# The opening of an adaLN linear-attention and bilinear-GLU block: loads on two issuers, sums moved between VectorE and TensorE, the k product by parts

## The chip, the cores and the metric

The kernel runs on one core of one Trainium2 chip. A core has TensorE (PE in the profile; PEld is its weight load), VectorE (DVE), ScalarE (ACT), GpSimd (POOL) and SyncE (SP), which issues the transfers in the kernel before. The engines run beside each other and wait for one another through semaphores; each works through its own instructions in the order in which the program gives them. The metric is the device time of one execution in microseconds, as the median of several runs; less is better.

## The reference, cut to what matters

The input x has 2048 tokens of width 512. One conditioning vector c makes six vectors of width 512, of which the first two are the shift `sa` and the scale `ca` of the first layer norm:

```python
mod = (_silu(c) @ w_mod).reshape(c.shape[0], 6, 1, -1)
sa, ca, ga, sb, cb, gb = (mod[:, 0], mod[:, 1], mod[:, 2], mod[:, 3], mod[:, 4], mod[:, 5])
h = _layernorm(x, axis=-1) * (1 + ca) + sa
x = x + ga * _A_ref(h, A_wqkv, A_wo)          # linear attention: q, k, v = h @ wqkv, 32 heads of 16
h = _layernorm(x, axis=-1) * (1 + cb) + sb
x = x + gb * _B_ref(h, B_w_gate, B_w_up, B_w_down)   # ((h W) * (h V)) W2
```

So before any product of h with `wqkv` can start, there must be the statistics of x, the normalized x, and the sums over 512 rows of `w_mod` that give shift and scale. All is float32.

## The kernel before, in words

Tokens are taken in 4 chunks of 512; a chunk is 4 tiles of 128 tokens by 512 columns (256 KB each). The 512 columns are 4 blocks of 128, called k (of the inner dimension) or b (of shift and scale). All products are made in three parts to keep float32's accuracy: each operand is split into a high part (a rounded copy, made by ScalarE) and a low part (the rest, made by VectorE), and the product is high by high, high by low, low by high.

The order of all work is written out by hand (`manual_schedule`): what stands earlier in the program comes earlier on its engine. The opening, lines 127 to 521, does this for chunk 0:

- Loads. `load` (L109) takes one of 99 buffers and issues a transfer from SyncE. The order is: x tile 0, c, x tiles 1 to 3, scale blocks 0 and 1 (`raw_half[1, 0]`, two transfers), shift blocks 0 and 1 (`raw_half[0, 0]`), the first block of the k weight, scale blocks 2 and 3, shift blocks 2 and 3, the other k weight blocks, then x of chunk 1, the q and v weights and the other chunks.
- Fillers. `keep_on` (L152) makes matmuls on zeros while nothing else is there for TensorE.
- Norm. `stats` (VectorE), `rstd_of` (VectorE, then GpSimd), `nmr_of` (VectorE) and `xhat` (ScalarE, for tile 3 VectorE) normalize a tile; `transpose_token` (L281) turns it on TensorE, 4 blocks of 128 by 128, into 4 banks, one for each k.
- Shift and scale. A block's 128 sums over 512 rows are made in one of two ways. `block_pe` (L390): 4 matmuls with one column each, straight from the loaded rows. `half_dve` (L397) with `mod_acc` (L167): 4 operations of VectorE over two blocks at once, after which `block_one` (L402) adds over the partitions by a matmul with ones. Before, scale blocks 0 and 1 go by `block_pe`, all others by `half_dve`. `block_out` (L407) takes a block's shift and scale out of PSUM on VectorE. Block 1's sums lie in the bank of the fillers (`ps_idle`), the others' in `ps_m`.
- h. `mod_h` and `mod_f` (ScalarE) make the modulated block k twice, rounded and full; `mod_l` (VectorE) the difference. `weight_h` (ScalarE) and `weight_l` (VectorE) split the k weight.
- k product. `cells` (L439) issues the matmuls of token tile t, block k and the parts asked for: part 0 is h high by weight high, part 1 h high by weight low, part 2 h low by weight high; 4 x 4 x 3 = 48 in all, into a bank for each t. The bank of t = 2 is `ps_idle`; that of t = 3 is one that the transposes of k = 0 had.

The lines that set the order of the first cells before are:

```python
half_dve(0, 0, 0, 1, 2, 3)
weight_h(0)
n0.transpose_token(2)
n0.transpose_token(3)
keep_on(2)
block_one(0, 0)
block_out(0)
weight_l(0)
mod_h(0)
```

After the opening, TensorE makes q, the k products of the other chunks and the attention's sums, and then the second half with its gate, up and down products.

Of the kernel before, what the change touches and what calls it, by code (L numbers as in the profile page):

```python
# [9 lines left out]
F32R = mybir.dt.float32r  # L10
AF = mybir.ActivationFunctionType
# [3 lines left out]
P = 128  # L15
# [7 lines left out]
def tile_adaln_block(  # L23
# [12 lines left out]
    nc = tc.nc  # L36
# [3 lines left out]
    KD = D // P  # L40
    NJ = 4
# [8 lines left out]
    xv = x[0].rearrange("(c p j) d -> c j p d", p=P, j=NJ)  # L50
# [14 lines left out]
    def f32(ap):  # L65
        return ap.bitcast(F32)
# [3 lines left out]
    def T(p, tag, shape=(P, D), dt=F32, bufs=None):  # L70
        cnt[0] += 1
        return p.tile(list(shape), dt, tag="t" if p is tiles else tag, name=f"{tag}_{cnt[0]}", bufs=bufs)

    def B(tag, shape=(P, D), dt=F32):

        return T(tiles, tag, shape, dt)
# [29 lines left out]
    nc.gpsimd.memset(half, -0.5)  # L106


    def load(src, tag):  # L109
        raw = B(tag, (P, *src.shape[1:]))[:src.shape[0]]  # L110
        nc.sync.dma_start(raw, src)
        return raw

    def load_x(ch):
        return [load(xv[ch, j], "x") for j in range(NJ)]

    def load_mod(v):
        return [load(wm_v[:, k, v * D:(v + 1) * D], "raw") for k in range(KD)]

    def load_half(v, half):  # L120
        a = v * D + half * D // 2
        return [load(wm_v[:, k:k + 2, a:a + D // 2], "raw") for k in range(0, KD, 2)]
# [3 lines left out]

    xts = [[load(xv[0, 0], "x")]]
    ct = consts.tile([P, KD], F32, name="ct")
    nc.sync.dma_start(ct, c[0].rearrange("(p k) -> p k", k=KD))
    xts[0] += [load(xv[0, j], "x") for j in range(1, NJ)]  # L130
    raw_half = {}
    raw_half[1, 0] = load_half(1, 0)
    raw_half[0, 0] = load_half(0, 0)
    load_k = lambda k: load(wqkv_v[k, :, D:2 * D], "raw")
    raw_k = [load_k(0)]
    raw_half[1, 1] = load_half(1, 1)
    raw_half[0, 1] = load_half(0, 1)
    raw_k += [load_k(k) for k in range(1, KD)]
    xts.append(load_x(1))
    raw_q = load_qkv(0)  # L140
    raw_v = load_qkv(2)
# [10 lines left out]
    def keep_on(n):  # L152
        for _ in range(n):
            nc.tensor.matmul(ps_idle, idle[:, :P], idle, start=True, stop=True)
# [12 lines left out]
    def mod_acc(acc, raws, ks):  # L167
        for k in ks:
            if k == 0:
                nc.vector.tensor_scalar(acc, raws[k], sc[:, 0:1], None, op0=ALU.mult)  # L170
            else:
                nc.vector.scalar_tensor_tensor(acc, raws[k], sc[:, k:k + 1], acc, op0=ALU.mult, op1=ALU.add)
# [148 lines left out]
    def k_split_xh(i):  # L321
        ch, j = divmod(i, NJ)
        kx[i] = [B("xh", dt=F32R), B("xl", dt=F32R)]
        nc.scalar.activation(kx[i][0], norm[ch].n[j], AF.Copy)

    def k_split_xl(i):
        ch, j = divmod(i, NJ)
        nc.vector.tensor_tensor(kx[i][1], norm[ch].n[j], f32(kx[i][0]), op=ALU.subtract)
# [45 lines left out]
    n0 = norm[0]  # L374
    both = consts.tile([P, KD, 2], F32, name="both")
    ca, sa = both[:, :, 0], both[:, :, 1]
    ps_m = acc_bank()

    def half_of(v, b):

        pair = raw_half[v, b // 2]
        return [pair[k // 2][:, k % 2, b % 2 * P:(b % 2 + 1) * P] for k in range(KD)]

    def at_of(v, b):
        return 2 * b + 1 - v

    def sums_in(b):
        return ps_idle if b == 1 else ps_m

    def block_pe(v, b):  # L390
        at, ps = at_of(v, b), sums_in(b)
        for k, raw in enumerate(half_of(v, b)):
            nc.tensor.matmul(ps[:, at:at + 1], raw, sc[:, k:k + 1], start=k == 0, stop=k == KD - 1)
# [3 lines left out]
    def half_dve(v, half, *ks):  # L397
        if 0 in ks:
            sums[v, half] = B("f")[:, :D // 2]
        mod_acc(sums[v, half], [raw_half[v, half][k // 2][:, k % 2] for k in range(KD)], ks)  # L400

    def block_one(v, b):  # L402
        at = at_of(v, b)
        nc.tensor.matmul(sums_in(b)[:, at:at + 1], sums[v, b // 2][:, b % 2 * P:(b % 2 + 1) * P], ones,
                         start=True, stop=True)

    def block_out(b):  # L407
        nc.vector.tensor_tensor(both[:, b], sums_in(b)[:, 2 * b:2 * b + 2], unit, op=ALU.add)

    halves = {}  # L410

    def mod_h(k):
        halves[k] = (B("h", dt=F32R), B("h", dt=F32R), B("f"))
        h, l, f = halves[k]
        nc.scalar.activation(h, n0.ps[k], AF.Identity, scale=ca[:, k:k + 1], bias=sa[:, k:k + 1])

    def mod_f(k, on=None):
        h, l, f = halves[k]
        if on:
            on.tensor_scalar(f, n0.ps[k], ca[:, k:k + 1], sa[:, k:k + 1], op0=ALU.mult, op1=ALU.add)  # L420
        else:
            nc.scalar.activation(f, n0.ps[k], AF.Identity, scale=ca[:, k:k + 1], bias=sa[:, k:k + 1])
        n0.ps[k] = None

    def mod_l(k):
        h, l, f = halves.pop(k)
        nc.vector.tensor_tensor(l, f, f32(h), op=ALU.subtract)
        n0.t[k] = (h, l)

    def weight_h(k):  # L430
        wk.append((B("w", dt=F32R), B("w", dt=F32R)))
        nc.scalar.activation(wk[k][0], raw_k[k], AF.Copy)

    def weight_l(k, on=None):
        (on or nc.vector).tensor_tensor(wk[k][1], raw_k[k], f32(wk[k][0]), op=ALU.subtract)
# [3 lines left out]
    def cells(*tk, parts=(0, 1, 2)):  # L439
        for part in parts:  # L440
            for t, k in tk:
                h, l = halves[k][:2] if k in halves else n0.t[k]
                x, w = ((h, wk[k][0]), (h, wk[k][1]), (l, wk[k][0]))[part]
                nc.tensor.matmul(kps[t], x[:, t * P:(t + 1) * P], w, start=k == 0 and part == 0,  # L444
                                 stop=k == KD - 1 and part == 2)
# [7 lines left out]
    n0.stats(2)  # L453
    n0.nmr_of(0, 2)
    n0.xhat(0, 1)
    k_split_xh(0)
    n0.stats(3)
    n0.rstd_of(2, 4)
    n0.transpose_token(0)
    n0.nmr_of(2, 4)  # L460
    n0.xhat(2)
    n0.xhat(3, on=nc.vector)
    keep_on(2)
    n0.transpose_token(1)
    block_pe(1, 0)
    keep_on(1)
    half_dve(0, 0, 0, 1, 2, 3)
    weight_h(0)
    n0.transpose_token(2)
    n0.transpose_token(3)  # L470
    keep_on(2)
    block_one(0, 0)
    block_out(0)
    weight_l(0)
    mod_h(0)
    mod_f(0)
    block_pe(1, 1)
    block_one(0, 1)
    half_dve(1, 1, 0, 1)
    block_out(1)  # L480
    half_dve(1, 1, 2, 3)
    mod_l(0)
    kps.update({t: acc_bank() for t in range(2)})
    kps[2] = ps_idle
    kps[3] = bank()
    four = lambda k: [(t, k) for t in range(NJ)]
    cells((0, 0), (1, 0), parts=(0, 1))
    cells((2, 0), (3, 0), parts=(0, 1))
    cells(*four(0), parts=(2,))
    mod_h(1)  # L490
    mod_f(1)
    weight_h(1)
    half_dve(0, 1, 0, 1, 2, 3)
    weight_l(1)
    mod_l(1)
    k_split_xh(1)
    cells(*four(1), parts=(0,))
    block_one(1, 2)
    block_one(0, 2)
    block_one(1, 3)  # L500
    block_one(0, 3)
    cells(*four(1), parts=(1, 2))
    weight_h(2)
    block_out(2)
    block_out(3)
    weight_l(2)
    mod_h(2)
    mod_f(2)
    weight_h(3)
    mod_l(2)  # L510
    mod_h(3)
    weight_l(3)
    mod_f(3)
    k_split_xl(0)
    mod_l(3)
    cells((0, 2), (1, 2))
    cells((2, 2))
    cells((0, 3))
    cells((3, 2))
    cells((1, 3))  # L520
    cells((2, 3))
    cells((3, 3))
    k_split_xl(1)
    nx = Norm(xts[1])

# [94 lines left out]
    for i in range(4, NT):  # L620
        ch, j = divmod(i, NJ)
# [910 lines left out]
```

## Time and profile before

| | |
|---|---|
| median of 3 runs | 556.27 us (556.25 to 557.45) |
| the profiled execution | 557.03 us, its span 555.0 us |
| TensorE busy | 547.7 us, 99% of the span |
| VectorE, ScalarE, GpSimd busy | 420.4, 296.0, 178.3 us |
| moved by transfers | 83.75 MB, 151 GB/s over the span |

In the profile, a line such as L444 is a line of the kernel; one helper's line stands for all its calls. A row of the timeline gives start, length, engine, line, operation, what is written and read, and in brackets the idle time of the engine before it and what ended that. Matmuls overlap with their successors, so their lengths (0.39 us for 512 columns) are longer than their spacing. The span is the profiler's; the execution's own time has 2.03 us more around it.

### The profile page before, as it was taken

Reading aid. Unit: us, or ns where it says so; the run is one execution under the profiler, and the core shown is the slowest. Engines: PE = TensorE matmul, PEld = TensorE weight load, DVE = VectorE, ACT = ScalarE, POOL = GpSimd, SP = SyncE. Lnnn points to the kernel's source line nnn. Section 1 sums busy time; section 2 is a strip of 40 time slices with the busy share of each in tenths; the row PEclk is TensorE's granted clock in tenths of the full one; section 3 lists DMA queues with packets and bytes.
Section 4 is the critical chain, followed back from the end, with each engine's and each line's share of the span. In section 5 each row is a group of like instructions: output and inputs, shape, how many; then the busy total and the mean of one; then the engine's idle time right before and its main releaser. Section 6 shows DMA issues by size and latency. Waiting matters only on the chain.

```text
span 555.0 us, 8026 instructions
## 1 busy us (share of the span) xinstructions
PE 547.7 (99%) x2739; PEld 459.8 (83%) x2739; DVE 420.4 (76%) x758; ACT 296.0 (53%) x525; POOL 178.3 (32%) x183
## 2 busy tenths in 40 slices
PE   8999999999999999999999999999999999999996
PEld 6788888888888888888888888878888888888886
DVE  5968779978898998865655767854567878778695
ACT  3876858546467876653545355432443535443540
POOL 2000000002627646343556644400512524242400
PEclk9999999999999999999999999999999999999999
DMA  8910224203230045185888635499585534342004
GB/s 261 384 38 1 76 77 151 78 0 77 77 115 2 0 149 192 39 298 196 284 283 268 227 123 199 154 379 327 176 275 178 185 119 146 131 147 72 0 1 152
DMA packets 56888, 83.75 MB, mean 151 GB/s; under 512 B 6736, under 2 KB 21840, under 8 KB 56848
## 3 DMA queue, kind: packets, MB, share of 16 engines
q1 hardware_dynamic: 56848, 83.26, 43.9%
q8 instruction: 21, 0.34, 0.2%
q14 instruction: 19, 0.16, 0.1%
HBM read 53.54 MB, written 29.69 MB: 150 GB/s over the span
## 4 chain that ended last, share of the span: by engine, by line
PE 96%; DMA 1%; DVE 1%; SPq 0%; issue 0%; ACT 0%; POOL 0%; DVEq 0%
PE bank L1023 38%; PE acc L1182 8%; PE acc L837 8%; PE bank L211 5%; PE bank L213 5%; PE bank L212 5%; PE acc L1106 4%; PE acc L1105 4%; PE acc L1107 4%; PE acc L362 3%; PE acc L361 3%; PE acc L360 3%; PE bank L276 2%; PE acc L444 1%; PE bank L812 1%; DMA x<-in_A_x_dram 1%
## 5 line engine op out<-in xcount | busy, mean ns | idle before, releaser
L1023 PE MATMUL bank<-h,w 128*128 128x512 f32 (+1 forms) x924 | 220.5, 392 | 0.0
L1023 PEld LDWEIGHTS bank<-h,w 128*128 128x128 f32 (+1 forms) x924 | 168.8, 186 | 36.5 <-issue 0.4
L1029 ACT ACTIVATE bank<-bank 128x512 f32<-128x512 f32 (+1 forms) x45 | 26.2, 581 | 131.3 <-PE bank L1023 131.0
L986 POOL TENSOR_TENSOR w<-raw,w 128x256 fp32r<-128x256 f32 (+3 forms) x22 | 24.2, 1099 | 79.7 <-ACT w L979 64.9
L1206 DVE TENSOR_TENSOR x<-acc,x 128x256 f32<-128x256 f32 x108 | 39.2, 414 | 10.5 <-PE acc L1182 9.9
L1182 PE MATMUL acc<-w,kh 128*128 128x256 f32 x252 | 46.8, 283 | 0.0
L211 PE MATMUL bank<-w,h 128*128 128x512 f32 x112 | 44.1, 394 | 0.0
L1182 PEld LDWEIGHTS acc<-w,kh 128*128 128x128 f32 x252 | 41.4, 191 | 3.1 <-DVE x L1206 0.2
L213 PE MATMUL bank<-w,h 128*128 128x512 f32 x112 | 43.7, 390 | 0.0
L212 PE MATMUL bank<-w,h 128*128 128x512 f32 x112 | 43.7, 390 | 0.0
L837 PE MATMUL acc<-w,xh 128*128 128x512 f32 x128 | 40.7, 399 | 0.0
L254 POOL TENSOR_TENSOR rstd<-ve,half 128x4 f32<-128x4 f32 (+3 forms) x12 | 11.2, 930 | 82.7 <-DVE ve L251 71.2
L1049 DVE TENSOR_TENSOR phi<-bank,g 128x512 f32<-128x512 f32 (+1 forms) x22 | 15.1, 687 | 29.8 <-PE bank L1023 28.3
L686 POOL TENSOR_TENSOR f<-h,zb 128x512 f32<-128x512 f32 x12 | 17.5, 1475 | 62.2 <-ACT zb L666 48.8
L1079 DVE TENSOR_TENSOR g<-bank,u 128x512 f32<-128x512 f32 (+1 forms) x22 | 15.2, 690 | 28.0 <-ACT u L1029 26.7
L1106 PE MATMUL acc<-w,kh 128*128 128x512 f32 (+1 forms) x92 | 35.9, 391 | 0.0
L1105 PE MATMUL acc<-w,kh 128*128 128x512 f32 (+1 forms) x92 | 35.9, 391 | 0.0
L1107 PE MATMUL acc<-w,kl 128*128 128x512 f32 (+1 forms) x92 | 35.8, 390 | 0.0
L1182 PE MATMUL acc<-w,kl 128*128 128x256 f32 x126 | 35.7, 283 | 0.0
L1029 ACT ACTIVATE u<-bank 128x512 f32<-128x512 f32 (+1 forms) x44 | 26.2, 594 | 12.6 <-PE bank L1023 12.4
L1112 DVE TENSOR_TENSOR x<-acc,x 128x512 f32<-128x512 f32 x44 | 28.0, 680 | 6.2 <-PE acc L1107 6.2
L269 ACT ACTIVATE n<-x,nmr,rstd 128x512 f32<-128x512 f32 x31 | 23.6, 808 | 14.2 <-DVE nmr L259 14.0
(195 smaller groups left out, 1186.8 us busy)
## 6 DMA issues: line engine op xcount, KB each, us to landing
right<-w SPq DMA_DIRECT2D x56, 256.0 KB, 3.8
w<-right SPq DMA_DIRECT2D x56, 256.0 KB, 3.7
x<-in_A_x_dram SPq DMA_DIRECT2D x24, 256.0 KB, 5.3
raw<-in_w_mod_dram SPq DMA_DIRECT2D x24, 256.0 KB, 3.6
raw<-in_B_w_down_dram SPq DMA_DIRECT2D x20, 256.0 KB, 3.1
side_s<-h SPq DMA_DIRECT2D x16, 256.0 KB, 2.8
h<-side_s SPq DMA_DIRECT2D x16, 256.0 KB, 6.0
raw<-in_A_wqkv_dram SPq DMA_DIRECT2D x12, 256.0 KB, 5.4
```

The lines of the kernel that those rows point to most:

```text
L211: nc.tensor.matmul(ps, ah, bh, start=begin and i == 0, stop=False)
L212: nc.tensor.matmul(ps, ah, bl, start=False, stop=False)
L213: nc.tensor.matmul(ps, al, bh, start=False, stop=end and i == n - 1)
L837: nc.tensor.matmul(yps[i], x, y, start=fresh and k + n == 0, stop=k == KD - 1 and n == 2, skip_group_check=True)
L1023: mm = lambda x, y, **kw: nc.tensor.matmul(ps, x[:, k], y, skip_group_check=True, **kw)
L1029: nc.scalar.activation(out, x, AF.Copy)
L1105: nc.tensor.matmul(dn[j], hh[:n, a:b], dh[:n], start=i == 0, stop=False)
L1106: nc.tensor.matmul(dn[j], hh[:n, a:b], dl[:n], start=False, stop=False)
L1107: nc.tensor.matmul(dn[j], hl[:n, a:b], dh[:n], start=False, stop=i == n_of - 1)
L1112: nc.vector.tensor_tensor(xt, dn[j], xt, op=ALU.add)
L1182: mm = lambda x, y, **kw: nc.tensor.matmul(ps, x[:, a:b], y, skip_group_check=True, **kw)
L1206: nc.vector.tensor_tensor(xt[:, halves[at]], banks[b][:, part], xt[:, halves[at]], op=ALU.add)
```

## The change

The edit is in the opening alone.

- Loads: c and x tiles 1 and 3 are issued by ScalarE, x tiles 0 and 2 and all else by SyncE. The second block of the k weight is moved ahead of shift blocks 2 and 3.
- Sums: shift blocks 0 and 1 are made by `block_pe` on TensorE, as scale's are, and `half_dve(0, 0, ...)` with its two `block_one` goes. For blocks 2 and 3, VectorE's first shift operation stands ahead of `mod_l(1)`.
- Order: block 0's sums stand ahead of the transposes of tiles 3 and 2, in this order; four of the fillers go; block 1's sums stand ahead of the first cells; the rounded copy of x tile 0 (`k_split_xh(0)`) moves behind the weights' copies.
- `mod_h` can do a part of the tokens; here it is called for all.
- k product: part by part over all four token tiles, for k = 0 and 1 and for parts 0 and 1 of k = 2; then, for each token tile, parts 0 and 1 of k = 3 and part 2 of k = 2 and 3.

```diff
-    def load(src, tag):
+    def load(src, tag, by=None):
         raw = B(tag, (P, *src.shape[1:]))[:src.shape[0]]
-        nc.sync.dma_start(raw, src)
+        (by or nc.sync).dma_start(raw, src)
         return raw
...
-    nc.sync.dma_start(ct, c[0].rearrange("(p k) -> p k", k=KD))
-    xts[0] += [load(xv[0, j], "x") for j in range(1, NJ)]
+    nc.scalar.dma_start(ct, c[0].rearrange("(p k) -> p k", k=KD))
+    xts[0] += [load(xv[0, j], "x", by=nc.sync if j == 2 else nc.scalar) for j in range(1, NJ)]
...
     raw_half[1, 1] = load_half(1, 1)
+    raw_k += [load_k(1)]
     raw_half[0, 1] = load_half(0, 1)
-    raw_k += [load_k(k) for k in range(1, KD)]
+    raw_k += [load_k(k) for k in range(2, KD)]
...
-    def mod_h(k):
-        halves[k] = (B("h", dt=F32R), B("h", dt=F32R), B("f"))
-        h, l, f = halves[k]
-        nc.scalar.activation(h, n0.ps[k], AF.Identity, scale=ca[:, k:k + 1], bias=sa[:, k:k + 1])
+    def mod_h(k, a=0, b=NJ):
+        if not a:
+            halves[k] = (B("h", dt=F32R), B("h", dt=F32R), B("f"))
+        h = halves[k][0][:, a * P:b * P]
+        nc.scalar.activation(h, n0.ps[k][:, a * P:b * P], AF.Identity, scale=ca[:, k:k + 1], bias=sa[:, k:k + 1])
...
     n0.xhat(0, 1)
-    k_split_xh(0)
     n0.stats(3)
     n0.rstd_of(2, 4)
     n0.transpose_token(0)
+    keep_on(1)
+    n0.transpose_token(1)
+    block_pe(1, 0)
+    block_pe(0, 0)
     n0.nmr_of(2, 4)
     n0.xhat(2)
     n0.xhat(3, on=nc.vector)
-    keep_on(2)
-    n0.transpose_token(1)
-    block_pe(1, 0)
-    keep_on(1)
-    half_dve(0, 0, 0, 1, 2, 3)
+    block_out(0)
     weight_h(0)
+    n0.transpose_token(3)
     n0.transpose_token(2)
-    n0.transpose_token(3)
-    keep_on(2)
-    block_one(0, 0)
-    block_out(0)
+    block_pe(1, 1)
+    block_pe(0, 1)
+    mod_h(0)
+    half_dve(1, 1, 0, 1)
     weight_l(0)
-    mod_h(0)
+    block_out(1)
     mod_f(0)
-    block_pe(1, 1)
-    block_one(0, 1)
-    half_dve(1, 1, 0, 1)
-    block_out(1)
     half_dve(1, 1, 2, 3)
     mod_l(0)
...
-    cells((0, 0), (1, 0), parts=(0, 1))
-    cells((2, 0), (3, 0), parts=(0, 1))
-    cells(*four(0), parts=(2,))
+    cells(*four(0), parts=(0,))
+    cells(*four(0), parts=(1, 2))
     mod_h(1)
+    weight_h(1)
+    weight_l(1)
     mod_f(1)
-    weight_h(1)
-    half_dve(0, 1, 0, 1, 2, 3)
-    weight_l(1)
+    half_dve(0, 1, 0)
     mod_l(1)
+    half_dve(0, 1, 1, 2, 3)
+    weight_h(2)
+    weight_h(3)
+    k_split_xh(0)
     k_split_xh(1)
     cells(*four(1), parts=(0,))
     block_one(1, 2)
+    block_one(1, 3)
+    cells(*four(1), parts=(1,))
     block_one(0, 2)
-    block_one(1, 3)
     block_one(0, 3)
-    cells(*four(1), parts=(1, 2))
-    weight_h(2)
+    cells(*four(1), parts=(2,))
     block_out(2)
     block_out(3)
     weight_l(2)
     mod_h(2)
+    mod_h(3)
     mod_f(2)
-    weight_h(3)
+    weight_l(3)
+    k_split_xl(0)
     mod_l(2)
-    mod_h(3)
-    weight_l(3)
     mod_f(3)
-    k_split_xl(0)
     mod_l(3)
-    cells((0, 2), (1, 2))
-    cells((2, 2))
-    cells((0, 3))
-    cells((3, 2))
-    cells((1, 3))
-    cells((2, 3))
-    cells((3, 3))
+    cells(*four(2), parts=(0, 1))
+    for t in range(NJ):
+        cells((t, 3), parts=(0, 1))
+        cells((t, 2), (t, 3), parts=(2,))
     k_split_xl(1)
```

## The prediction

> **What bounds the kernel now.** I read the page first: busy time and the chain that ended last.
>
> ```profile
> span 555.0 us, 8026 instructions
> PE 547.7 (99%) x2739; PEld 459.8 (83%) x2739; DVE 420.4 (76%) x758; ACT 296.0 (53%) x525; POOL 178.3 (32%) x183
> PE 96%; DMA 1%; DVE 1%; SPq 0%; issue 0%; ACT 0%; POOL 0%; DVEq 0%
> ```
>
> TensorE is the bound, but this share is a mean. So the second view is the busy time by stretch: fillers while the first loads come, transposes and sums, the k product of the first four token tiles, and the rest (stretch and length, then busy time and count of PE, PEld, DVE, ACT, POOL, then clock, DMA share, GB/s).
>
> ```profile
> 2.00:8.56 6.56, 6.55 (x18) 4.90 (x18) 3.46 (x12) 1.15 (x4) 1.36 (x8) 1.00 0.81 249
> 8.56:14.66 6.10, 5.67 (x42) 4.78 (x42) 4.49 (x12) 3.45 (x6) 0.70 (x1) 1.00 1.09 371
> 14.66:27.20 12.54, 12.42 (x58) 9.86 (x57) 11.51 (x25) 10.23 (x18) 0.00 (x0) 1.00 1.05 384
> 27.20:550.30 523.10, 523.06 (x2625) 440.25 (x2623) 399.29 (x707) 279.97 (x500) 174.95 (x166) 1.00 0.42 142
> ```
>
> From 27.20 to 550.30 PE is busy in 523.06 of 523.10 us, and the change touches nothing there. So the time changes by what the end of the k product at 27.20 is moved, one for one. Ahead of it, what counts is the chain in order of time (start, length, what):
>
> ```profile
> 2.65 5.93 DMA x<-in_A_x_dram
> 8.60 0.71 DVE st L242
> 10.73 0.82 ACT n L269
> 11.60 1.09 PE bank L283 x8
> 25.31 1.37 PE acc L444 x6
> ```
>
> The fourth x tile lands at 2.65 + 5.93 = 8.58; its statistics start at 8.60, its normalization and that of tile 2 at 10.73, their 8 transposes at 11.60. Steady cells of the k product take 1.37 / 6 = 0.228 us each.
>
> **The loads.** SyncE's issues, then two answers on single loads, the second half of the shift's first blocks (call it w00b) and the first part of w11a (scale, blocks 2 and 3), with the time from issue to landing:
>
> ```profile
> 0.80 0.38 SPq L111 DMA_DIRECT2D x<-in_A_x_dram  x1
> 1.24 0.42 SPq L129 DMA_DIRECT2D ct<-in_c_dram  x1
> 1.71 1.37 SPq L111 DMA_DIRECT2D x<-in_A_x_dram  x3
> 3.12 1.97 SPq L111 DMA_DIRECT2D raw<-in_w_mod_dram  x4
> ...
> L111 SPq DMA_DIRECT2D raw<-in_w_mod_dram x1: 469/469/469, 4.6 to 4.6; - x1
> DMA to landing us min/median/max: 7.0/7.0/7.0
> ...
> L111 SPq DMA_DIRECT2D raw<-in_w_mod_dram x1: 531/531/531, 5.9 to 5.9; - x1
> DMA to landing us min/median/max: 7.1/7.1/7.1
> ```
>
> w00b lands at 11.6, w11a at 13.0. What computes with them, and the fillers (timeline: start, length; brackets hold idle time and its releaser):
>
> ```profile
> 0.80 1.28 ACT L161 ACT_TABLE_LOAD   x1 [0.80 <-PEq L1518]
> 4.10 0.20 ACT L161 ACTIVATE ce<-ct 128x4 f32<-128x4 f32 x1 [2.02 <-DMA ct<-in_c_dram]
> 9.12 0.61 ACT L324 ACTIVATE xh<-n 128x512 fp32r<-128x512 f32 x1
> 12.30 0.63 ACT L432 ACTIVATE w<-raw 128x512 fp32r<-128x512 f32 x1 [0.76 <-DMA raw<-in_A_wqkv_dram]
> 13.83 0.78 ACT L415 ACTIVATE h<-bank,both 128x512 fp32r<-128x512 f32 x1 [0.89 <-DVE both L408]
> 20.03 0.78 ACT L415 ACTIVATE h<-bank,both 128x512 fp32r<-128x512 f32 x1 [1.72 <-DVE both L408]
> ...
> 7.50 0.16 DVE L259 SCALAR_TENSOR_TENSOR nmr<-mv,rstd 128x2 f32<-128x2 f32 x1
> 11.19 0.35 DVE L170 TENSOR_SCALAR f<-raw,sc 128x256 f32<-128x256 f32 x1
> 11.57 1.52 DVE L172 SCALAR_TENSOR_TENSOR f<-raw,sc,f 128x256 f32<-128x256 f32 x3
> 13.63 0.16 DVE L408 TENSOR_TENSOR both<-acc,unit 128x2 f32<-128x2 f32 x1 [0.54 <-PE acc L404]
> 16.15 0.68 DVE L427 TENSOR_TENSOR h<-f,h 128x512 fp32r<-128x512 f32 x1
> ...
> 1.98 6.58 PE L154 MATMUL acc<-w 128*128 128x512 f32 x18 [1.98 <-DVE w L149]
> 9.96 0.95 PE L393 MATMUL acc<-sc,raw 128*128 128x1 f32 x8
> 14.66 1.43 PE L444 MATMUL acc<-w,h 128*128 128x512 f32 x5
> 18.84 0.95 PE L404 MATMUL acc<-ones,f 128*128 128x1 f32 x8
> 27.20 0.39 PE L211 MATMUL bank<-w,h 128*128 128x512 f32 x1
> ```
>
> The chain into the first cell at 14.66: four sums of shift on VectorE (11.19 to 13.09), a matmul with ones, the sum taken out (13.63), h (13.83, 0.78 us).
>
> **The change, term 1: the order of work, with every load landing as now.** Block 0's shift goes to TensorE ahead of the transposes: 4 matmuls of 0.95 / 8 = 0.12 us, the last two behind w00b at 11.6, so done by about 12.0. Tiles 3 and 2 are then transposed, 8 in 1.09 us, to 12.9 (now 12.7: this wait puts transposes behind a load). ScalarE copies the weight at 12.30 to 12.93, and h starts at once: 12.95 + 0.78 = 13.73. Block 1's 8 sums (0.95 us) fill PE until 13.85, and the first cell starts there, 0.8 sooner than 14.66.
>
> From there the product takes 12.54 us now: 48 x 0.228 = 10.9, 8 matmuls with ones 0.8 (0.95 less an overlap), 0.8 of waits and restarts. After: 10.9, four such matmuls 0.45, and these waits. The third cell writes the bank that holds block 1's sums, so it waits for VectorE to take these out, and VectorE has first w11a's two sums (13.0 + 0.35 + 0.51), a weight's low part (0.68): 14.55, and 0.16 to 14.7, where the cell was due at 14.3: 0.4. The low part of h: two more sums (1.0) and 0.68 after 14.7 is 16.4, due at 14.75 + 6 x 0.228 = 16.1: 0.3. Blocks 2 and 3 are finished by VectorE about 3 us later (0.68, 0.35, 0.68, three sums of 0.51), while PE has 12 cells and 2 sums in hand, 3.0 us; then h of 2 (0.16 + 0.78) stands against four cells (0.9): 0 to 0.3. The last low part: 0 to 0.3. That and five restarts of some 0.1 make 1.45. Together 12.8, so the end is 13.85 + 12.8 = 26.65: **term 1 is -0.55 us**, and I take -0.5.
>
> **Term 2: the loads.** x tiles 1 and 3 and ct go to ScalarE's queue. The fourth x tile is its third issue and goes out at about 0.80 + 2 x 0.45 = 1.7, not 2.65; SyncE reaches w_mod as its third load, at 1.7 and not 3.12. What landings gain is not in the trace. Low end: nothing, if the DMA engines and not the issues are late (a loss of 0.3, if the first x tile shares them with the second; VectorE's 0.94 us between 7.66 and 8.60 would cover it). High end: the stage from 2.00 to 8.56 moves 249 GB/s where the next moves 371; at that rate its bytes take 4.4 us, 2.15 less. I take the row that is nearest, the x issue: 2.65 - 1.7 = 0.95, and call it 0.9. All that bounds term 1 (w00b, w11a, the weight) moves with it until the normalization is late instead: the fourth tile's statistics can't start before 7.66, 0.94 sooner, so transposes end no sooner than about 11.8 and the first cell starts no sooner than 12.8. With loads that early the third cell's 0.4 is gone too, the product takes 12.4 and ends at 25.2: both terms together give -2.0 at most, -2.3 with what my working may be off. **Term 2: -0.9.**
>
> **At nothing:** Four fillers go (0.9 us at 0.23): they lay in waits. Three issues on ScalarE (1.3 us) and the table load (1.28) end at 3.4, before ct's exponential at 4.10; would the table load go first, the issues would begin at 2.08 and term 2 would be near nothing. Copying x tile 0 (0.61) moves from 9.12 to behind the fourth weight, into the 1.72 us that ScalarE waits ahead of 20.03. The second k weight passes two loads of shift on SyncE's queue; each of these is one load later (0.7 us) but is wanted only after 16.8. Beyond 27.20 VectorE is busy 399 of 523 us and gets its inputs sooner too.
>
> **Sum.** -0.5 - 0.9 = -1.4. The profiled execution took 557.03 us (span 555.0 and 2.03 around it), so it would take 555.6; the median of the runs is 556.27, 0.76 below it, and goes to **554.9**.
>
> **Rivals.** *Loads land no sooner* (under 0.5 us): for it, one issuer keeps 371 and 384 GB/s in the later stages, and SyncE's 0.42 us per 256 KB is faster than that; against it, this says nothing of the first 6 us. Only term 1 and a remnant are left: 555.3 to 556.1, about 555.8. [...]
>
> *Loads land over 1.2 us sooner*: two queues fill the gap between 249 and 371 GB/s, and the normalization bounds the start: gains of 1.7 to 2.3, 554.0 to 554.6, about 554.3. For it: the DMA share of 0.81 in the first stage.
>
> *The clock falls, and it ends slower.* The change leaves one filler of five in the stretch before the first cell, and PE some 1 us more of waits and single-column matmuls there. Fillers by stretch (busy and count of PE, then PEld), and the clock at the end:
>
> ```profile
> 2.50:6.70 4.20, 4.20 (x11) 3.26 (x10) 1.00 0.80 238
> 6.70:8.50 1.80, 1.80 (x8) 1.16 (x7) 1.00 0.92 291
> ...
> 553.00:555.00 2.00, 0.00 (x0) 0.00 (x0) 0.00 (x0) 0.00 (x0) 0.00 (x0) 0.50 0.02 5
> ```
>
> Until 6.7 a filler takes some 0.42 us, after it 0.23: PE starts slow and is let go after 4.7 us of work. If it fell back ahead of the cells, 4.7 us at that rate would lose 4.7 x (1 - 0.228/0.42) = 2.15, and -1.4 becomes +0.75: 557.0. It decides from any fall longer than 3 us. Against it: the fall at the end came over 2 us after the last matmul, and the longest wait after is under 1 us. [...]
>
> **Chances.** Forecast (loads 0.5 to 1.2 sooner, 554.6 to 555.3) 0.37; loads over 1.2 sooner 0.36; loads no sooner 0.18; clock 0.09. What a measurement of this kernel tells from no change is about 0.3%, 1.67 us, so faster means under 554.6: the second case, 0.36. The forecast, the loads no sooner and nearly half of the clock case (0.04) lie within: 0.59. Slower, above 557.9, needs the clock case without term 2 (+2.15 - 0.5): 0.05. The range 553.9 to 556.4 holds the three cases with both ends of term 2 and leaves out the clock's 0.09 and tails of 0.05.
>
> **What would show it.** Fourth x tile landed near 7.6 (no sooner: 8.4 or later; much: below 7.0); first cell near 13.0; end of the product near 25.8; a wait of the third cell for the take-out of block 1; spacing of cells 0.23 from the first on (clock case: 0.43). The prediction is wrong if any load of w_mod or of the weight lands later than now, if ScalarE's issues come after its table load, or if PE waits again beyond the product.

## The result and the profile after

The changed kernel takes 561.33 us (median of 21 runs, 557.35 to 562.82), the one before 556.8 us beside it: 1.0072 times as long, 95% interval 1.0059 to 1.0084. So it is slower by 0.7%, where 0.3% faster was forecast. What happened is the rival to which the prediction gave 0.09: the clock fell.

The busy time by stretch of the changed kernel, with the columns of the prediction's second view (length, then busy time and count of PE, PEld, DVE, ACT, POOL, then clock, DMA share, GB/s); the granted clock changes at 13.88 and 20.70, the k product ends at 30.76, and the two stretches ahead of 13.88 are each half as long as the 6.82 us at half clock:

```profile
7.05:10.46 3.41, 2.61 (x14) 1.84 (x14) 2.34 (x10) 1.52 (x2) 1.41 (x2) 1.00 1.09 376
10.46:13.88 3.42, 3.42 (x34) 3.42 (x32) 1.95 (x6) 2.00 (x3) 0.00 (x0) 1.00 1.08 362
13.88:20.70 6.82, 6.82 (x23) 5.85 (x23) 4.57 (x11) 4.82 (x9) 0.00 (x0) 0.50 1.06 387
20.70:30.76 10.06, 10.03 (x48) 7.79 (x46) 6.72 (x14) 6.08 (x11) 0.00 (x0) 1.00 0.77 284
```

From 13.88 to 20.70 the clock stands at 0.50. In the stretch just ahead of that, PE is busy all the time, 3.42 of 3.42 us: nothing in the busy column warns of the fall. What PE does there is seen in these rows of the timeline (start, length, operation; brackets: idle time before and its releaser):

```profile
9.52 0.66 PE L284 MATMUL bank<-ident,n 128*128 128x128 f32 x4 [0.80 <-ACT n L270]
9.93 0.47 PE L155 MATMUL acc<-w 128*128 128x512 f32 x1
10.24 0.64 PE L284 MATMUL bank<-ident,n 128*128 128x128 f32 x4
10.72 1.84 PE L394 MATMUL acc<-sc,raw 128*128 128x1 f32 x16
12.43 1.07 PE L284 MATMUL bank<-ident,n 128*128 128x128 f32 x8
13.34 2.91 PE L394 MATMUL acc<-sc,raw 128*128 128x1 f32 x16
16.11 1.63 PE L446 MATMUL acc<-w,h 128*128 128x512 f32 x3
30.76 0.39 PE L212 MATMUL bank<-w,h 128*128 128x512 f32 x1
```

The one filler ends at 10.40; from there to the fall there are only single-column sums and short transposes. Each matmul of a sum stands as two instructions in the rows, so a row of 16 is scale and shift of one block. The second such row takes 2.91 us where the first takes 1.84, because the clock goes from 1.00 to 0.50 in its midst, at 13.88. The first cell starts at 16.11 (before 14.66) and the product ends at 30.76 (before 27.20), 3.56 us later. The span is 4.3 us longer. Of the other 0.7 us, 0.4 are two waits of PE far behind the opening, which end at 137.85 and 157.99; for the rest no wait is seen. The same stretch behind the product took 523.8 us here, 523.1 before, 523.84 in a variant of the kernel before (the run with wide sums in place of its fillers) and 523.07 in a variant of the changed kernel (the run with wide sums), so that part is not put down to the change.

The loads did come sooner. SyncE's issues in the changed kernel's timeline:

```profile
0.80 0.85 SPq L111 DMA_DIRECT2D x<-in_A_x_dram  x2
1.71 2.83 SPq L111 DMA_DIRECT2D raw<-in_w_mod_dram  x4
```

ScalarE's in the same view, with its table load and its normalizations:

```profile
0.80 0.41 ACTq L129 DMA_DIRECT2D ct<-in_c_dram  x1
1.24 0.93 ACTq L111 DMA_DIRECT2D x<-in_A_x_dram  x2
2.20 1.28 ACT L162 ACT_TABLE_LOAD   x1 [2.20 <-issue]
8.65 1.52 ACT L270 ACTIVATE n<-x,nmr,rstd 128x512 f32<-128x512 f32 x2 [4.27 <-DVE nmr L260]
10.65 0.81 ACT L270 ACTIVATE n<-x,nmr,rstd 128x512 f32<-128x512 f32 x1 [0.48 <-DVE nmr L260]
```

And the answers on two loads, the second half of the shift's first blocks (w00b) and x tile 1, with the time from issue to landing:

```profile
L111 SPq DMA_DIRECT2D raw<-in_w_mod_dram x1: 368/368/368, 4.2 to 4.2; - x1
DMA to landing us min/median/max: 5.9/5.9/5.9
...
L111 ACTq DMA_DIRECT2D x<-in_A_x_dram x1: 450/450/450, 1.2 to 1.2; - x1
DMA to landing us min/median/max: 5.2/5.2/5.2
```

w00b lands at 4.2 + 5.9 = 10.1, 1.5 us sooner, and the fourth x tile at 7.8, 0.8 sooner. But x tile 1 lands at 6.4, and its statistics started at 5.48 before. So the first normalization starts at 8.65 and not 7.69, and that of tiles 2 and 3 at 10.65, next to the 10.73 of before.

### The profile page after: what moved, and what is told of

Read it like the earlier page. It is cut to its first block, busy times and chain, and to the rows that moved or that the text cites. A ratio compares the mean times of both kernels' runs of the same rounds, so it can differ in the third digit from the quotient of the medians.

```text
span 559.3 us, 8036 instructions
## 1 busy us (share of the span) xinstructions
PE 551.3 (99%) x2747; PEld 462.9 (83%) x2747; DVE 420.7 (75%) x754; ACT 295.7 (53%) x525; POOL 177.7 (32%) x183
## 4 chain that ended last, share of the span: by engine, by line
PE 92%; DVE 4%; ACT 2%; DMA 1%; issue 0%; POOL 0%; ACTq 0%; DVEq 0%; POOLq 0%
PE bank L1020 38%; PE acc L1179 8%; PE acc L834 8%; PE acc L1102 4%; PE acc L1103 4%; PE acc L1104 4%; PE bank L212 4%; PE bank L214 4%; PE bank L213 4%; PE acc L363 2%; PE acc L361 2%; PE acc L362 2%; PE acc L446 2%; PE bank L277 2%; PE bank L809 1%; DMA x<-in_A_x_dram 1%
```

## The experiments

All ratios are against the kernel before, run beside them on the same chip.

| run | ratio (95%) | runs with mean clock of 0.996 or less | first cell, end of product |
|---|---|---|---|
| e1, loads alone | 1.0001 (0.9993 to 1.001) | 0 of 12 | 14.76, 27.28 |
| e2, changed, one issuer | 1.0075 (1.0057 to 1.0093) | 6 of 6 | 16.22, 30.43 |
| e3, before with fewer fillers | 1.0044 (1.0027 to 1.0061) | 6 of 6 | 14.86, 29.42 |
| e4, changed with six fillers more | 1.0039 (1.0027 to 1.0051) | 0 of 5 | 16.32, 28.96 |
| e5, before with single-column fillers | 1.0022 (1.0005 to 1.0038) | 9 of 12 | 15.54, 30.02 |
| e6, before with sums on TensorE | 1.0013 (0.9995 to 1.0032) | 2 of 12 | 15.29, 27.52 |
| e7, changed with shift on VectorE | 1.0006 (0.9997 to 1.0014) | 0 of 11 | 14.44, 27.36 |
| e8, as e7, sums in a gap | 1.0000 (0.9985 to 1.0014) | 0 of 11 | 15.27, 28.15 |
| e9, changed with wide sums | 1.0000 (0.9991 to 1.0010) | 0 of 11 | 14.94, 27.70 |
| e10, e6 with wide sums, no fillers | 0.9998 (0.9986 to 1.0009) | 0 of 12 | 14.46, 26.80 |
| e11, e3 with wide sums | 1.0003 (0.9992 to 1.0014) | 0 of 12 | 14.58, 27.09 |

A mean clock of 0.996 or less is read as a fall: the four profiled runs with 6.82 us at half clock have 0.992 or 0.993, all other profiled ones 0.997 or more. Of the changed kernel's 21 runs, 18 had a mean clock of 0.993 or less; the three others (0.998 and more) took 557.35, 557.8 and 558.26 us. The kernel before is not quite free of falls either: 3 of the 81 runs beside these experiments have 0.996 or less, and one of the 21 beside the changed kernel took 561.5 us, its clock not on record.

**Which part: loads, fillers?** e1 is the kernel before with the change of issuers alone:

```diff
-    nc.sync.dma_start(ct, c[0].rearrange("(p k) -> p k", k=KD))
-    xts[0] += [load(xv[0, j], "x") for j in range(1, NJ)]
+    nc.scalar.dma_start(ct, c[0].rearrange("(p k) -> p k", k=KD))
+    xts[0] += [load(xv[0, j], "x", by=nc.sync if j == 2 else nc.scalar) for j in range(1, NJ)]
```

(`load` gets its argument `by`, as in the change.)

> The kernel before with c and x tiles 1 and 3 issued by ScalarE, nothing else changed. Clock theory (the changed kernel is slow because the granted clock falls to half from 13.88 to 20.70 us, after a stretch of single-column matmuls with one filler in it): the three fillers of the stretch are all there, the clock stays at 1.00, and the time is within 0.3% of before; the fourth x tile lands near 7.8 and the w_mod loads some 1.3 us sooner, and the first cell starts 0 to 0.5 us sooner than 14.66. Load theory (the second x tile, which lands at 6.42 in the changed kernel and not at 5.46, holds up the normalization): the first transposes start near 9.5 and not 8.56, and the time is 0.5 us or more longer.

It came out at 1.0001, so two issuers give and cost nothing. Its timeline on VectorE (statistics of the four x tiles; the first starts at 4.16 and the second at 6.49, each after a wait for its load; then the sums of block 0 taken out):

```profile
4.16 0.69 DVE L242 BATCH_NORM_STATS2 st<-x 128x6 f32<-128x512 f32 x1 [2.24 <-DMA x<-in_A_x_dram]
6.49 0.69 DVE L242 BATCH_NORM_STATS2 st<-x 128x6 f32<-128x512 f32 x1 [0.82 <-DMA x<-in_A_x_dram]
7.51 0.69 DVE L242 BATCH_NORM_STATS2 st<-x 128x6 f32<-128x512 f32 x1
8.58 0.69 DVE L242 BATCH_NORM_STATS2 st<-x 128x6 f32<-128x512 f32 x1
13.74 0.16 DVE L408 TENSOR_TENSOR both<-acc,unit 128x2 f32<-128x2 f32 x1 [0.68 <-PE acc L404]
```

The statistics of the fourth tile start at 8.58, as before at 8.60: what was a wait for its load is now the queue of three statistics behind x tile 1. So the first transposes start at 9.56 and not 8.56, as the load theory had it, but the first cell only 0.1 later than before (14.76), and the time is no longer; the gain of up to 0.5 us that I had thought possible is not there either.

e2 is the changed kernel with every load on SyncE (`by=nc.sync`, and ct too):

> The changed kernel with every load issued by SyncE. Clock theory: the same stretch of single-column matmuls, so the clock falls here too, and the time stays 0.5% to 1% above before. Load theory: back to within 0.3% of before.

It was as slow as the changed kernel, so the issuers have no part in the loss. e3 takes fillers from the kernel before:

```diff
     n0.xhat(3, on=nc.vector)
-    keep_on(2)
...
     n0.transpose_token(3)
-    keep_on(2)
```

> The kernel before without the two keep_on(2) of the stretch between 8.56 and the first cell, so with one filler there as in the changed kernel. [...] Order theory (the clock falls because of the 16 more single-column matmuls, not for lack of fillers): the clock stays at 1.00 and the time is that of before within 0.2%.

```profile
9.90:13.31 3.41, 2.86 (x25) 2.46 (x23) 2.56 (x8) 1.49 (x3) 0.14 (x1) 1.00 1.10 363
13.31:20.14 6.83, 6.83 (x22) 5.67 (x22) 5.95 (x14) 4.45 (x7) 0.00 (x0) 0.50 1.06 385
```

The stretches of e3: the half clock is there, as long as in the changed kernel. Without these four fillers of 0.23 us the clock fell in 6 of 6 runs; with them, in the kernel before, in 3 of 81. e4 gives them back to the changed kernel, six in number:

```diff
     block_pe(1, 0)
+    keep_on(2)
     block_pe(0, 0)
+    keep_on(2)
...
     n0.transpose_token(3)
+    keep_on(2)
     n0.transpose_token(2)
```

> The changed kernel with six fillers more: two behind each of block 0's two sums and two between the transposes of tiles 3 and 2. They cost up to 6 x 0.23 = 1.4 us of PE. Clock theory: the clock stays at 1.00, the half clock's loss (about 3.2 us: 11 cells at 0.43 and not 0.23, 10 sums at 0.21 and not 0.11) is gone, and the k product ends at 28 to 29 and not at 30.8, so 558.5 to 560. Order theory (the sums on TensorE alone are the cost): 560 or more, as the changed kernel or above it.

The clock held in all five runs and 1.8 us came back in the profile (30.76 to 28.96). The fillers' own 1.4 us stayed, since PE has no wait left there to hide them (it is busy 6.95 of 6.95 us from 9.37 to 16.32).

**Busy, or streaming?** e5 is meant to keep PE as busy as before, but with single columns:

```diff
-    keep_on(2)
+    narrow(2)     # matmul(ps_idle[:, :1], idle_f[:, :P], idle_f[:, :1]), float32
```

at both places of e3.

> The kernel before with the two keep_on(2) of the stretch between 8.56 and the first cell replaced by four float32 matmuls of a single column on the same bank, about 0.23 us each like the fillers, so that PE is as busy as before. Activity theory (what holds the clock is columns that stream through the array, and single-column matmuls count for little): the clock falls to half as with fewer fillers, 0.3% to 0.6% slower. Idle theory (what lets the clock fall is time in which PE does nothing): the clock stays at 1.00 and the time is that of before within 0.2%.

These are the stretches of e5, ahead of its fall and at half clock, and then the like stretch of the kernel before:

```profile
10.37:13.78 3.41, 2.80 (x23) 2.44 (x23) 2.44 (x7) 1.44 (x2) 0.25 (x1) 1.00 1.10 365
13.78:20.61 6.83, 6.83 (x22) 5.77 (x22) 6.07 (x14) 4.45 (x7) 0.00 (x0) 0.50 1.05 386
...
10.09:13.50 3.41, 2.98 (x23) 2.26 (x21) 2.42 (x6) 1.45 (x2) 0.41 (x1) 1.00 1.10 358
```

It fell in 9 of 12 runs, and the kernel before beside it in 2 of 35. The loss, 0.22%, is less than I had expected, as some runs were spared and some mean clocks (0.994 to 0.996) point to a shorter fall. Two of its fillers take 0.50 us in the timeline, two of before 0.72, and PE was busy 2.80 of 3.41 us ahead of the fall, where the like stretch of the kernel before has 2.98. So e5 alone would leave some room for idle time as the cause; the changed kernel's 3.42 of 3.42 doesn't. e9 is the changed kernel with the same number of matmuls, none added, and 128 equal columns in each sum:

```diff
+    scw = B("f").rearrange("p (k c) -> p k c", k=KD)
...
+        nc.vector.tensor_copy(scw, sc.unsqueeze(2).to_broadcast([P, KD, P]))
...
-            nc.tensor.matmul(ps[:, at:at + 1], raw, sc[:, k:k + 1], start=k == 0, stop=k == KD - 1)
+            nc.tensor.matmul(ps[:, at:at + P], raw, scw[:, k], start=k == 0, stop=k == KD - 1)
```

(`at_of` and `block_out` follow the wider places.)

> The changed kernel, in which each matmul that makes a block's sums from the loaded rows has 128 equal columns of silu(c) as its moving operand and not one; one column of the result is used. No filler is added, and one copy on VectorE makes the columns. Column theory (the gate counts columns that stream through the array): the clock stays at 1.00 in most runs, and if the matmuls cost no more than now (0.115 us an instruction, as the transposes of 128 columns do), the time is that of the changed kernel's runs without the fall, 557.3 to 558.3. Rival (only 512-column or single-pass matmuls hold the clock): it falls as before, 560 to 562. If the wide matmuls are slower, the first cell is later by 32 times the difference.

```profile
9.37 0.66 PE L286 MATMUL bank<-ident,n 128*128 128x128 f32 x4 [1.33 <-ACT n L272]
10.57 1.95 PE L396 MATMUL acc<-f,raw 128*128 128x128 f32 x16
13.23 1.95 PE L396 MATMUL acc<-f,raw 128*128 128x128 f32 x16
14.94 0.99 PE L449 MATMUL acc<-w,h 128*128 128x512 f32 x3
27.70 0.39 PE L214 MATMUL bank<-w,h 128*128 128x512 f32 x1
```

These are rows of its timeline: the transposes of one tile, the sums, the first cells and the end of the product. Its stretches, up to the first cell and then the product:

```profile
8.90:14.94 6.04, 5.57 (x50) 5.44 (x50) 2.74 (x9) 3.90 (x6) 0.70 (x1) 1.00 1.08 368
14.94:27.70 12.76, 12.75 (x59) 9.69 (x58) 11.02 (x23) 10.12 (x18) 0.00 (x0) 1.00 1.04 383
```

Sixteen instructions of wide sums take 1.95 us, sixteen of single-column ones 1.84, next to nothing more. The clock held in 11 of 11 runs, and the time is that of the kernel before. That is the whole loss undone by one width: with the same number of matmuls the clock fell in 18 of 21 runs with one column in each sum, PE busy 3.42 of 3.42 us, and in none of 11 with 128. One reservation: e9, e10 and e11 ran on another chip than e2 to e6. The clock fell on both chips that e2 to e6 used, but the narrow sums with few fillers were not run on the third, so there the comparison is between chips; e3 and e4, and e5 and the kernel before, are on the same chip. e11 shows the same on the kernel before (e3 with the same width):

> The kernel before without its two keep_on(2), which lost 0.44% with the clock at half, now with the sums that it makes on TensorE (scale, blocks 0 and 1) at 128 equal columns. Column theory: the clock holds in most runs, and the time is that of before within 0.15%. Rival: it falls, 0.3% to 0.5% above.

The falls went from 6 in 6 runs to none in 12, and the time is that of before (1.0003).

**The sums' own cost.** e6 is the kernel before with shift blocks 0 and 1 on TensorE and its five fillers:

```diff
-    keep_on(1)
-    half_dve(0, 0, 0, 1, 2, 3)
+    block_pe(0, 0)
+    keep_on(1)
...
-    block_one(0, 0)
...
-    block_one(0, 1)
+    block_pe(0, 1)
```

> The kernel before with the sums of shift blocks 0 and 1 on TensorE and no other part of the change: loads, fillers and the order of the product are those of before. Theory (PE has no room there: 16 single-column instructions more at 0.115 us are 1.84 us, less 4 with ones, 0.46, less some 0.4 of idle time): the product ends 0.9 to 1.4 us later with the clock at 1.00, about 0.2% slower, and if the clock falls too another 2 to 3 us. Rival, the forecast's step (the sums fill waits, and VectorE is rid of 1.9 us): the first cell starts sooner than 14.66 and the time is 0 to 0.2% less.

```profile
8.84:15.29 6.45, 6.45 (x53) 6.16 (x54) 2.43 (x7) 4.02 (x6) 0.70 (x1) 1.00 1.08 373
15.29:27.52 12.23, 12.23 (x58) 9.83 (x58) 11.06 (x23) 9.61 (x17) 0.00 (x0) 1.00 1.05 386
```

PE has no wait left in either stretch. The first cell is 0.63 later, the product 0.31 shorter (12.23 for 12.54, probably since VectorE is rid of work), the end 0.32 later: less than I had expected, and no measured difference. e7 is the changed kernel with the shift back on VectorE and five fillers:

```diff
-    keep_on(1)
+    keep_on(2)
...
-    block_pe(0, 0)
+    keep_on(1)
...
-    block_out(0)
+    half_dve(0, 0, 0, 1, 2, 3)
...
+    keep_on(2)
+    block_one(0, 0)
+    block_out(0)
     block_pe(1, 1)
-    block_pe(0, 1)
+    block_one(0, 1)
```

> The changed kernel with the sums of shift blocks 0 and 1 back on VectorE and the five fillers of before; its loads, the place of the second k weight and the order of the product by parts stay. Theory (sums on TensorE and the clock are the whole loss): within 0.15% of before, clock at 1.00. Rival (the order of the product costs too): 0.2% or more above before with the clock at 1.00.

At 1.0006 the order of the product by parts costs nothing that these runs can tell. Two tries at a faster kernel: e8 (e7 with `half_dve(0, 0, 0, 1)` ahead of `nmr_of(2, 4)` and without the last two fillers) and e10 (e6 with the wide sums and no filler in the stretch).

> As the run with the shift's sums back on VectorE, but its first two sums stand in the gap in which VectorE waits for GpSimd's power (9.7 to 10.5), which the earlier loads allow, and the last two fillers are left out. [...]

> The kernel before with the sums of shift blocks 0 and 1 on TensorE, the same 128 equal columns, and none of the five fillers of the stretch. Column theory: the clock stays at 1.00, and five fillers of 0.23 us are gone from a stretch in which PE never waits: the first cell starts near 14.2 and not 15.3, the product ends near 26.5 to 27, and the time is 0.1% below before to equal. Rival: the clock falls, 0.4% to 0.7% above before.

In e8, with three fillers in the stretch, the clock held in all 11 runs, but in its profile the first transposes waited 2.44 us for a late x tile, and the median is that of before. PE stood idle longer there than ahead of any fall in a profile (0.8 us at most). In e10, with no filler in the stretch, the clock held in all 12 runs. The product ends at 26.80, 0.4 sooner, and PE hardly waits; its ratio of 0.9998 shows no gain.

## Why the prediction was wrong

- *The clock, priced under the rivals.* This is the step that failed. I set against it that the clock at the end fell only over 2 us after the last matmul (2.5 us, from 550.33 to 552.8), and that the longest wait would be under 1 us: I took idle time for what counts. It fell with PE busy for 3.42 of 3.42 us. In e8 it held in all 11 runs, with PE idle for 2.44 us in the profile. The price that I gave the rival, 2.15, was too low: 6.82 us at half rate, and not 4.7, lose 6.82 x (1 - 0.228 / 0.427) = 3.2; the product ended 3.06 later than in e9, in which the clock held.
- *Four fillers at nothing, since "they lay in waits".* Wrong in the same way. What they did shows in the clock, not in PE's time: without them it fell in 6 of 6 runs (e3).
- *Term 1, the sums.* I read the row of 8 instructions as 8 matmuls, scale and shift of a block; they are one of the two, since each of the 4 matmuls of `block_pe(1, 0)` stands as two instructions. Scale and shift of a block take 1.84 us on TensorE and not 0.95, and the changed kernel does that for two blocks. With the clock held (e9) the first cell starts at 14.94, and not near 13.0, and the product ends at 27.70: term 1 and term 2 together are +0.5 in the profile, and not -1.4, with no difference in the measured times. So the forecast would have missed with the clock held too: 0.3% faster lies outside e9's interval.
- *Term 2, the loads.* The w_mod loads came 1.5 us sooner, more than the 0.9 that I took, and it bought nothing. For x tile 1 I had allowed a loss of 0.3, an estimate of mine that no run shows, which VectorE's 0.94 us of waiting would cover; tile 1 came 0.9 us later, which used up just that. So the rival "loads land no sooner" was wrong on the loads and right that they bring nothing. For the first w_mod load the landing followed the issue: it was issued 1.41 us sooner (1.71 for 3.12) and landed 1.3 sooner, 6.3 us behind its issue and 6.2 before. But w00b landed 1.5 sooner though its own issue came only 0.4 sooner (4.2 for 4.6); why, no run shows. For the time it is all one: e1 came out at 1.0001.
- *ScalarE's issues stand ahead of its table load* (2.20), and PE passes on one for one what the opening loses (3.56 us at the end of the product, 3.6 of the span's 4.3): both as forecast. That all waits beyond the opening stay as they were held but for the 0.7 us above, which came and went between profiles.
- *The wait of the third cell* for the take-out of block 1 was forecast at 0.4; in e9 the first three cells take 0.99 us, where three in the steady run take 0.85, so at most 0.14 of it is there.

What stays open: what part the transposes had in the fall, and how wide the sums have to be for the clock to hold here. No run varied the transposes, or took a width between 1 and 128 columns. Nor is it shown why some runs of a kernel fall and others don't.

## What to carry to other kernels

Ahead of a dense part, look at what PE does in the stretch that leads to it and not only at whether it is busy: here it was busy 3.42 of 3.42 us with single-column sums and transposes, the clock fell to 0.50, and the product ended 3.06 us later than with the clock held (e9). Where such sums are needed, try 128 equal columns instead of adding fillers: the clock held in all 35 runs of e9, e10 and e11, and sixteen instructions took 1.95 us for 1.84. When an early load is moved to a second queue, look at which other load then lands later (here x tile 1, by 0.9 us), and at what comes next in the queue of the engine that waits for it.

## What the runs showed of the hardware that I had not expected

The granted clock fell to 0.50 with PE busy 3.42 of 3.42 us, stayed there for 6.82 us in this kernel and as long in three others (13.31 to 20.14 in e3, 12.97 to 19.79 in e2, 13.78 to 20.61 in e5), and came back to 1.00 within the k product, 3.6 to 5.3 us after its first cell (4.6 in this kernel: 16.11 to 20.70). Other runs seem to have fallen for longer: of the changed kernel's 18, the 8 with a mean clock of 0.992 or 0.993, as the profiled one, have a median of 560.7 us, and the 10 with 0.989 to 0.991 one of 562.1. By my estimate from these means (0.003 of 560 us, halved clock) that is about 3 us more at half clock; none of these was profiled. Sixteen float32 matmul instructions on 128 columns took 1.95 us, on a single column 1.84. And the fall does not come in every run of one and the same kernel: 3 runs of the changed kernel's 21, and 3 of e5's 12, were spared.
